# Another recorded order of the tasks in a two-layer recurrent-memory transformer, with the x blocks asked for ahead of the first V weights

## The chip, the cores and the metric

The kernel runs on one core of one Trainium2 chip. The metric is the device time of one execution in microseconds (us); lower is better. The core has five engines that run their own instruction streams in order and wait for each other by semaphores: PE (TensorE, matrix products; its weight loads are listed apart as PEld), DVE (VectorE), ACT (ScalarE), POOL (GpSimd) and SP (SyncE). DMAs are asked for ("issued") by SP and by POOL here, and are carried out by 16 DMA engines that both share. SP and POOL are queues too: an instruction that has to wait holds up everything behind it on its engine.

## The reference

All tensors are bf16. With x of 2048 rows by 512 columns, the output is

```
x = x + A(layernorm(x));  x = x + B(layernorm(x))
x = x + A(layernorm(x));  x = x + B(layernorm(x))      # the same weights again
```

A is an attention with a recurrent memory. The rows are cut into 64 segments of 32. For each segment in turn, 8 memory rows and the segment's 32 rows form h (40 rows); each of 32 heads of 128 columns has q = h Wq, k = h Wk, v = h Wv, p = softmax of the masked q k / sqrt(128), o = p v; the heads' o times Wo gives 40 rows, of which the first 8 are the memory of the next segment and the other 32 the output. So the segments follow one another strictly. B is a gated layer: (sigmoid(x w_gate) * (x w_up)) w_down with 1792 inner columns. Wq, Wk, Wv and Wo have 4.2 MB each.

## The kernel before

**Steps.** The two attention layers run interleaved: step t (0 to 69) treats segment t of layer 1 and segment t-6 of layer 2 (names `j` = 0 and 1). Steps 0 to 5 have layer 1 alone, with 40 columns of h and 14 columns of layer 2's first x rows beside them. A step is built by `emit_step`. Its heads are taken in groups g0 to g5 of 6, 6, 6, 6, 6 and 2. Per group: **QK** (line 868, matrix products of 3 heads' q and k at a time, two such halves `w0` and `w3`), a cast of it to SBUF on ACT (`qku`), **SC** (line 904, the scores), the softmax (DVE lines 918, 923, 925, ACT line 928 with the exponential, DVE lines 930, 932, 939), **PTR** (line 950, transposes of p), copies on ACT or DVE, **PVM** (line 976, p times v), a cast on ACT (`otsb`), and **WO** (line 995, times Wo, adding into one bank for the whole step). At a step's end DVE copies the new memory rows into the next step's h (line 1008), and only then can the next step's QK start.

**V.** v of the x rows is not made in the step. Each block of 128 x rows (16 blocks, 4 segments each) is normalised (`layernorm_T`, lines 582 to 595: statistics and scaling on DVE, one power on POOL, a transpose on PE), and a **V pass** (line 635: four matrix products of 512 columns with one eighth of Wv, "piece" 0 to 7) makes 128 rows by 4 heads of v. The result is cast by ACT or DVE to a staging buffer, written to a scratch in DRAM (`scr`, line 1224 on SP or POOL) and read back per step into `vsb`. The 16 or so rows that depend on the memory, or lie next to it, are made inside the step by **strips** (line 762, 32 matrix products of 512 columns, of which four run at once in column groups); these are cast to `sst` and moved by DMA to `vsb`. Blocks 2, 3, 4, 5, 7, 8, 10, 11, 13 and 14 are done ahead ("boot"), so V passes are the work that PE has while it waits for weights or for a softmax.

**Weights.** `load_weights` asks on SP for Wv in 8 pieces of 512 KB, for Wq and Wk in 6 pieces each (heads 0-2, 16-18, 3-8, 19-24, 9-15, 25-31) and for Wo in 12. Piece k of Wv is asked for only when piece k-2 has landed (`tk.after`). w_gate, w_up and w_down of the gated layer (`wg`, `wu`, `wd`) come by POOL, 256 KB at a time.

**Order.** A planner holds some 14,000 tasks. It does not decide the order: the order is recorded in a packed text, `SEQUENCE` (line 53), together with one bit for every task that two engines can do (ACT or DVE for a copy, SP or POOL for a DMA):

```
code = lzma.decompress(base64.b85decode("".join(SEQUENCE.split())), ...)
left = list(range(len(T)))
order = [T[left.pop(q)] for q in struct.unpack_from(f"<{len(T)}H", code)]
...
    tk.on = tk.eng[code[2 * len(T) + k // 8] >> k % 8 & 1]
self.replay(order)
```

`replay` goes through that order with the planner's own durations. From it come which buffer a task gets, which PE task a 256 KB load on POOL waits for (`pace`), and where `warm` puts filler matrix products (line 1214, tile `hot`) into the bank of a task that the planner expects late. `run` (line 1199) then emits the tasks in that order; each engine's stream is the order cut to its tasks.

Of the kernel before, what the change touches and what calls it, by code (L numbers as in the profile page):

```python
# [1293 lines left out]
```

## Time and profile before

| | |
|---|---|
| median of 3 runs | 1747.63 us |
| lowest and highest | 1746.31 and 1748.25 us |
| profiled execution | 1747.1 us from its first to its last instruction, clock granted in full |
| PE busy | 1733.4 us (99%) |
| DVE, ACT, POOL busy | 1248.4 (71%), 1128.5 (65%), 859.0 us (49%) |
| DMA | 273.41 MB, mean 156 GB/s; 285 and 320 GB/s in the first two fortieths of the span |

The page gives no time of the profiled execution other than its span; the span is 0.5 us under the median of the runs. In the tables of the profile "x12" is a number of instructions, "L635" a line of the kernel, `bank<-wv_sb,xvf` what is written from what. Matrix products overlap, so that a busy PE is not yet a PE at its full rate: what counts is the distance from one start to the next, for example 32 products of 512 columns in 7.07 us (line 635 at 13.28 us), that is 0.216 us each.

### The profile page before, as it was taken

The numbers are of one execution on the slowest core, as the hardware profiler recorded it, in microseconds if no ns is written. First come the engines' busy times: TensorE is split into PE (matmuls) and PEld (weight loads), VectorE is DVE, ScalarE is ACT, GpSimd is POOL, SyncE is SP. The second block draws the span as 40 slices with busy tenths as digits, with TensorE's granted clock in tenths as the row PEclk, the third lists the DMA queues.
The fourth block names the chain that finished last, engine by engine and source line by source line (L and its number), as shares of the span: only waits on it lengthen the run. The fifth ranks groups of instructions, "written<-read, shape, count | busy, mean of one in ns | idle before, by whom it ended". The sixth has DMA issues, their size and how long they took to land.

```text
span 1747.1 us, 91842 instructions
## 1 busy us (share of the span) xinstructions
PE 1733.4 (99%) x39162; PEld 1491.8 (85%) x39162; DVE 1248.4 (71%) x4208; ACT 1128.5 (65%) x3119; POOL 859.0 (49%) x1367
## 2 busy tenths in 40 slices
PE   9999999999999999999999999999999999999998
PEld 4688789889898988989888888989888888988886
DVE  5677777677767776786777767776777776767676
ACT  3576777566666766666666666666665666666564
POOL 5624345635544554445445554544455364454543
PEclk9999999999999999999999999999999999999999
DMA  8935355645645555545555464545455464554644
GB/s 285 320 100 155 109 151 161 195 113 153 174 130 163 156 159 143 165 125 164 152 148 158 136 184 128 166 138 153 132 174 166 139 174 128 144 156 131 178 120 134
DMA packets 145583, 273.41 MB, mean 156 GB/s; under 512 B 39686, under 2 KB 86018, under 8 KB 145174
## 3 DMA queue, kind: packets, MB, share of 16 engines
q0 software_dynamic: 72944, 198.79, 39.8%
q1 hardware_dynamic: 72230, 68.75, 13.3%
q8 instruction: 307, 5.03, 1.2%
q14 instruction: 102, 0.84, 0.2%
HBM read 221.78 MB, written 27.07 MB: 142 GB/s over the span
## 4 chain that ended last, share of the span: by engine, by line
PE 94%; DMA 3%; DVE 1%; SPq 1%; issue 1%; POOL 0%; ACT 0%; POOLq 0%; ACTq 0%
PE bank L868 34%; PE bank L995 17%; PE bank L1097 12%; PE bank L762 8%; PE bank L635 6%; PE bank L1120 6%; PE bank L904 4%; PE bank L976 4%; PE bank L950 2%; PE bank L595 1%; PE bank L1214 1%; DMA wk_sb<-in_A_Wk_dram 1%; DMA wo_sb<-in_A_Wo_dram 0%; PE bank L1065 0%; DMA scr<-wu 0%
## 5 line engine op out<-in xcount | busy, mean ns | idle before, releaser
L868 PE MATMUL bank<-hT,wq_sb 128*128 128x80 bf16 (+3 forms) x8960 | 616.4, 198 | 1.0 <-DVE hT L1008 0.3
L868 PE MATMUL bank<-hT,wk_sb 128*128 128x80 bf16 (+3 forms) x8960 | 616.3, 198 | 0.8 <-DMA wk_sb<-in_A_Wk_dram 0.6
L1228 ACT CAST qku<-bank 128x480 bf16<-128x480 f32 (+4 forms) x770 | 384.7, 508 | 223.7 <-PE bank L868 194.6
L868 PEld LDWEIGHTS <-wq_sb 128*128 128x128 bf16 x8960 | 454.2, 99 | 32.1 <-issue 15.1
L868 PEld LDWEIGHTS <-wk_sb 128*128 128x128 bf16 x8960 | 446.9, 99 | 1.1 <-DMA wk_sb<-in_A_Wk_dram 0.7
L995 PE MATMUL bank<-otsb,wo_sb 128*128 128x80 bf16 (+1 forms) x8960 | 360.2, 198 | 2.2 <-DMA wo_sb<-in_A_Wo_dram 1.3
L918 DVE TENSOR_TENSOR st<-bank,cst 40x240 f32<-40x240 f32 (+3 forms) x768 | 280.5, 368 | 113.2 <-PE bank L904 97.5
L995 PEld LDWEIGHTS <-wo_sb 128*128 128x128 bf16 x8960 | 336.6, 99 | 15.5 <-DMA wo_sb<-in_A_Wo_dram 2.0
L1228 ACT CAST otsb<-bank 128x480 bf16<-128x480 f32 (+3 forms) x420 | 200.2, 483 | 83.4 <-PE bank L976 52.8
L1090 POOL DMA_DIRECT2D wu<-in_B_w_up_dram x217 | 166.5, 768 | 170.0 <-PE bank L950 36.4
L1114 POOL DMA_DIRECT2D wd<-in_B_w_down_dram x217 | 156.9, 723 | 182.0 <-PE bank L1120 39.6
L1224 POOL DMA_DIRECT2D vsb<-sst x351 | 178.2, 512 | 129.6 <-ACT sst L1228 64.7
L1089 POOL DMA_DIRECT2D wg<-in_B_w_gate_dram x217 | 166.4, 767 | 138.1 <-PE bank L1097 56.7
L928 ACT ACTIVATE st<-st 80x240 f32<-80x240 f32 (+3 forms) x420 | 159.2, 381 | 58.0 <-DVE st L925 54.8
L1097 PE MATMUL bank<-xnT,wg 128*128 128x128 bf16 (+2 forms) x1784 | 171.5, 218 | 0.0
L1097 PE MATMUL bank<-xnT,wu 128*128 128x128 bf16 (+2 forms) x1784 | 171.1, 218 | 0.0
L930 DVE TENSOR_REDUCE small<-st 80x6 f32<-80x240 f32 (+3 forms) x420 | 151.5, 363 | 23.4 <-ACT st L928 20.2
L1220 ACT ACTIVATE ptsb<-bank,small 120x160 bf16<-120x160 bf16 (+3 forms) x430 | 156.6, 386 | 17.2 <-PE bank L950 10.7
L904 PE MATMUL bank<-qku 128*128 128x80 bf16 (+1 forms) x2240 | 162.7, 197 | 1.0 <-issue 0.9
L925 DVE TENSOR_TENSOR st<-st,small 80x240 f32<-80x240 f32 (+3 forms) x420 | 155.0, 370 | 5.7
L939 DVE TENSOR_TENSOR pb<-st,small 80x240 bf16<-80x240 f32 (+3 forms) x420 | 154.1, 370 | 5.7
L923 DVE TENSOR_REDUCE small<-st 80x6 f32<-80x240 f32 (+3 forms) x420 | 152.5, 364 | 6.2
(108 smaller groups left out, 2554.1 us busy)
## 6 DMA issues: line engine op xcount, KB each, us to landing
wg<-in_B_w_gate_dram POOLq DMA_DIRECT2D x220, 256.0 KB, 4.2
wu<-in_B_w_up_dram POOLq DMA_DIRECT2D x220, 256.0 KB, 4.2
wd<-in_B_w_down_dram POOLq DMA_DIRECT2D x220, 256.0 KB, 3.9
vsb<-scr SPq DMA_DIRECT2D x137, 66.0 KB
scr<-vst SPq DMA_DIRECT2D x90, 96.0 KB
vsb<-scr POOLq DMA_DIRECT2D x93, 66.0 KB, 3.4
vsb<-sst SPq DMA_DIRECT2D x179, 32.0 KB
vsb<-sst POOLq DMA_DIRECT2D x169, 32.0 KB, 2.8
```

What stands on the lines that cost most here:

```text
L868: nc.tensor.matmul(o_ap, lhsT=W[:, c, h * P:(h + 1) * P], rhs=mv(c), start=(c == 0), stop=(c == DC - 1))
L904: nc.tensor.matmul(s_all(SB)[:, w0 + i, :], lhsT=fview(qku[:, i, 0, 0:1], [(1, P)]), rhs=qku[:, i, 1, 0:ncol], start=True, stop=True)
L918: pl.add("DVE", dve_ns(n, True), lambda gsz=gsz, hs=hs, st=st, SB=SB, pj_=pj_, npj_=npj_, mk=mk, idx=idx: nc.vector.tensor_tensor(out=st[p ...
L928: pl.add("ACT", act_ns(n), lambda hs=hs, st=st: nc.scalar.activation(out=st[pr, hs], in_=st[pr, hs], func=ACTF.Exp, scale=self.scale), r=s ...
L995: nc.tensor.matmul(WB[:, c * ncol:(c + 1) * ncol], lhsT=self.wo[:, h, c * P:(c + 1) * P], rhs=otsb[:, hl, 0:ncol], start=(h == 0 and c == ...
L1089: pl.add("POOL", 760, lambda wg=wg, fs=fs: nc.gpsimd.dma_start(out=wg[:], in_=self.wgv[:, :, fs]), r=[("wo", self.H - 1)], w=[gk] + bt, la ...
L1090: pl.add("POOL", 760, lambda wu=wu, fs=fs: nc.gpsimd.dma_start(out=wu[:], in_=self.wuv[:, :, fs]), r=[("wo", self.H - 1)], w=[uk] + bt, la ...
L1097: nc.tensor.matmul(gu[:, 2 * i + k, 0:n], lhsT=W[:, c, i * P:(i + 1) * P], rhs=xnT[:, c, rw], start=(c == 0), stop=(c == DC - 1))
L1114: pl.add("POOL", 760, lambda wd=wd, ip=ip: nc.gpsimd.dma_start(out=wd[:], in_=self.wdv[:, 2 * ip:2 * ip + 2, :]), w=[dk] + (["boot"] if se ...
L1220: nc.scalar.activation(out=dst, in_=src, func=ACTF.Copy, scale=by)
L1224: {"SP": nc.sync, "POOL": nc.gpsimd}[tk.on].dma_start(out=got[1], in_=got[2])
L1228: nc.scalar.copy(out=dst, in_=src)
```

## The change

Nothing but the text `SEQUENCE` differs: 92 lines of packed text become 88.

```
 SEQUENCE = r"""
-;BKuib6o%lfB&)8j78VFm3*TORJaEeTpTegcj@45cPG=tDu9Cop`gL7BsLuS#OcT}UGbOE%Rvw4_#4%#$D8H!O&97}fvKE=gc~
...
+-XmYACJ&^@_Q*%Pqd)VfD(Os7%#QMrvJwasc?e7tW4e|DX`7=(P4&9b1jfW|}nyY`GtB?m|%9YiB{%_E6Z!fQiku2zXKR#fd!bV
...
 """
```

Both texts unpack to an order of the same 13,976 tasks, and can be compared as lists:

- **Where.** Only the front differs. On PE the last 3750 of 4202 tasks stand in the same order; the first of them is a task of step 7 that starts at 205.84 us in the profile. The other engines' orders agree from about the same place on. 191 tasks change their engine: 50 DMAs go from SP to POOL, 36 from POOL to SP, 59 copies from ACT to DVE, 46 from DVE to ACT.
- **The first requests on SP** (x4 is block 4 of x, 128 KB; v0 is piece 0 of Wv, 512 KB; m the memory rows; q, k, o pieces of Wq, Wk, Wo by heads; S a write of v to the scratch):

```
before  v0 x4 x3 v1 x14 x2 v2 m v3 x0 v4 v5 x5 v6 S x11 x7 v7 x8 x10 q16-18 x1 S S q0-2 x13 S k0-2 k16-18 S S S S q25-31 ...
after   x4 x3 x14 x2 v0 x5 v1 v2 x0 v3 v4 x11 v5 v6 x7 (mask) v7 m x1 x10 q0-2 x13 S S k16-18 x8 S S S S q25-31 S k0-2 S S q16-18 ...
```

- **Weights.** MB asked for ahead of a piece (SP and POOL together, in the recorded order), and the PE work recorded ahead of its first use (number of matrix products times their distance in the profile; fillers not counted):

| piece | MB ahead, before | after | PE work ahead, before (us) | after (us) |
|---|---|---|---|---|
| v6 | 3.94 | 4.06 | 10.40 | 11.49 |
| v7 | 4.79 | 4.72 | 13.22 | 13.44 |
| q 16-18 | 5.78 | 9.84 | 31.63 | 32.08 |
| q 25-31 | 9.22 | 7.90 | 41.05 | 39.92 |
| k 3-8 | 17.11 | 16.98 | 47.88 | 48.79 |
| o 0-2 | 19.56 | 18.83 | 54.49 | 59.29 |
| o 28-30 | 23.05 | 23.06 | 62.57 | 65.16 |

  On SP 24 writes of v stand ahead of most Wo pieces before, and 17 to 19 after. The first piece of Wo of 384 KB is the 61st request on SP before, and the 55th after. The V writes of the strip that is done ahead for block 0 stand from place 32 on before, behind q 16-18, q 0-2, k 0-2 and k 16-18; after, the first stands at place 30, behind q 0-2 and k 16-18 alone.
- **V passes.** In PE's order the V passes of block 13 with pieces 0, 1 and 2 stand in step 1 before and in step 0 after, so that step 0 has 23 V passes for 20, and step 1 none for 3. Steps 2 and 3 keep three and two. Two transposes of the layer norm stand at the end of step 3 before; after, one stands at the end of step 2 and one within step 3.
- **Start.** On DVE the first block's scaling stands behind the statistics of the second block before, and behind those of the second and third after. On POOL six clearings of buffers stand ahead of the first power after, none before.
- **Step 1.** On DVE a cast of a strip stands inside the step's softmax instructions before; after, ACT has it, and DVE has one cast to `kx` (0.23 us for this kind in the profile) inside them.
- **Step 7.** Of the 18 DMAs that fill its `vsb`, 10 are on POOL before and 8 on SP; after, 6 and 12. Between them on POOL stand five 256 KB loads for the gated layer before (issued at 201.21 to 208.02 us), of which four stand further ahead after.

More of the change, by code (lines that the diff above doesn't have):

```diff
@@ new lines @@
+!(`Ye}I4@U$IQaXEDjRGy!`PtL<i9-G13$hzV;?YvxzU_S%nj>}5AQt<$S)u+*SpZ(LQM?zaW5{YqNmQd}nP$PmtFilvq1+MOc7%LF6`h89JsjYs{wA_7TQq#b=5HArnYUIM?S_dSG4<lx0EcBu9?D*W=p`L%*#6#G{VU`^b>?vuPW
+6FiQT0!o_J)`NB!&iWBJ7<-7W26m&)A{(k@T2PFDvwsi1<s;*OJ`cXJRspxb{AL}sBs<zM;vt6=4K+>$M1I={iIvqlt;m6<6NWG@c)WETY9+BE#O0H_t}=!myNXLLQCJ6+lj*5Z6sp>5l4ztM>LwnwdZ_#_EfBSEupcg*~zZ_QFM{)
+@`HP}1mfWJ0>Za_618ryvEIm*?v4sbyAHTO(4kRDNRWZ@6+6HSX&@pw0wB*@7xHfjY!|*acCX;aw$amNxA|6z2{v6~8fECFmNK3b&14Ofrsv1G;1qZn5cXO*>>Y5$+tT}K-96&O*xgT#msf(}43%&knWSPq*tfFRMX0D42q5u6fm2Q
@@ new lines @@
+LK`)`+63>On?wcKGu@zlif|B$FN#s6_lh@`FBkq<2Kb=Rhobh6`>F;T=i{w`3ywB-Qn`W?HbZ8CD(aEXXj{H4Fa9z48>;ovo4<kBuXA0n09Gv<4!-;r-yn9{%3>_OA5nENe1<B8ep#imFD|F6_Hr+^Twxu33RbWVk(XASy!a2{f-Tr
+AW>b|eXpw9D3&Nv}IgL}6bp8e=^7LiWRNL}ne&9H^&vDTVBW&bC4lOp_zv$9pMGX^avS%vNsquy;Zv$oUjjlzC73v4AraD#(9BGH|&;4x*8q3v<*`G=Qyq)KZ)2Q0>5Hq8k6CdC6F@3je=4i^|R14i$+`wjMgqIDu>{W&!IuPGnUo7
+gdB(33EB4OT7HC@m0{tU}|JN5(0|bv<kS%65vr#%lByC;<^lXa4if%*c(t3QQ!etqPsja}hd|olAFRtln#FduWYJp^9UTJw%KJS7~L8u+@x@%)*aKMW@tw#pX;We%UBo7+{m0cCt%KL=b9;1aH0&*{}?0@+pAGYaJ}az!hHz*<%pZN
@@ new lines @@
+pr4VF;F-%N(THuG?YdD#XXT<2S_yx4uOccUb0Gj5+o~e$2X@v&);U$VhSbpmwxSnfrZmYbSrptcr&c6Sr9%|#CMAIX70;Q<&cf%G1t764=dvGUkcA*U{mDl++gsubaC;Qy4qrDF+u*61pBa-=#-x{6Rn&Q5cNo~jJ4~D;+1ZOyep`g
+U)34u>l986h48THSR)W)v5GJ|Op&V-2_nbH3@n;2Rl^;|T#B|6T5{}t>oBItCzxen&U7cpt<-j~{cQ8H7XCC~c+49JGV0PV<l51B892ThAs4!KvFJSB+w)us>=`JX9hO{ec%~0HwI>!Mg!I6tj`4@qkI2{+&NLS>{lbCVIi@`&96OC
+Ksd7Bz;<T>}3gcss26gO8$hFDw{<^a2$Mi=YC=}}I5qyxo2%4oZR*~ih<gzzy(t|yE)oo?)QPzOY6A9*bOg&{6V$#_AoR>+Q{G&(e%4ot=S{R>J0s0Lj(YN%yZV}dxK3l$ExEJ7^A(I?WC1aHJs$ENz#IFFh&k8pB)C%N5+H<t9O~L
+)KNW2jj<l|%33G-f=+r1mSr#pe`t_fK*-LdH`cdg>DqJIUV4`5GgsewM4l}UI_)VS8qk>^>CFuH5jemNW+vGQP;$dU78GZ6Z`3>^33wEc|@W8IoN>02q}hAE>=M^l=Vg+nKqh>-n84zHRiGI%?DXFH$s%3=<q#WvG5Mj-wVA>4kQd7
@@ new lines @@
+E03qH%+7lEbuG6>X$)nTif;glWDfcr%_t<yVSGzte(o?dg|VaP^Tb$|kiqvHfy6jB=owPwa<Pfk5`9R~^mH2A$obd@{uKt_-nVge&An&Glpq98)I%lixOVlKLxmi7atClf*WkE!>E*y>Pw268owasqt!;Rs1*dV2?WIX9sIlCBx90f
+1}DRp@r7FcGRnw`Jj)!=TjlL3S~6HDwZCCtM*p7hS_2wCt*rKVOZ8a`)U^F4$^Z~rUi|KBDHh}_2!-eH1nezsg7_$$9G<l6luG_<=%RqdpQFoj<QViy}XZh)c&hk(=6vqPrX{pQ31G1pzd>u20KD=?OT}$T?MUIZm{8trMaMXK=d40
+4F4?tj+LeJDjAAJO&@DVXL{%~gJ$Y+Cr`z`)vxh566DphvD6X;ZV*>4Dj^QtkoYE}#zyL7Rwu*xjA(I71j~LgMdaPn%1mV9?%3wgUar^*b#k)=qaYM(R}USBBS?&uT_CNd&fUJl5N`{mFwx_)Bep`E!{Zwik@{k-pNw1ri5&o3sGd%
@@ new lines @@
+oIch|Z^k9B<)JD8i50euasKL0-2nwG<{V;o+qlz_)qhSD2wj?OZA@Z=n#3<=SVpsWcqRQ!ieZ+W8j*5DSF0^+fovKte0yt<@fpUq_HtCfYwzTxL;L+~xetKx{uISdgfiYq{Dfv4%V5)zn*>dFaT1NTPGfyx%F<^50zfA399^#v|=oY
+JS;vS#7uNj?OTI711f_)k{Q4vs(i7pE*vQL>`7rO$QdS2Lb{*O+28Nktw^?a7^R{M<>wu{lkuTbt7?^o@hoef^L8f<8yv@j0Ge{)f4ZQZG^l@h%wt+W$jJ!S893L7{gA#G!NQG-APtD*|S{)a!JSjxNTIRie5b`T#{ykncPBCLBa9_
+etRG8<caqUs2`DaijyvXz-C9l~pJE8gery6H4APFM)W*fr{>@)X%+?n@>s8{GilrF!Ei6aMoEynJAF8fmwp2$B+vzYXtsBCy&HybpBnuMsMx-D|dgM@7~4&BaZv5i5^JEIm$=YWY^A0u>bsT+j`kAGB5qi*QzGAxYmQ$`caYl456T3
@@ L145 @@
+Jcd+-{c%-Eou@Wp{BtK{_Pl_en!PErvz@amS1+`ykBNt^=2cKl{L9VQ*deej!w02=K6_B-QHHsvzLjv5vAj86<ukdVK`0o?0$%k{AO=ps#3!%bxi_<JIU7li63j0^_G=vFOX0ntNZaTWax;FXW&$U{V&TyHd0%cy;QUXQ-Z~Nb+cW-
+p6DcpO{b2Iuy>_{GhWQj9ENV&WP2iTHn%|5z9Q)z*(fa1M&L(Pvm)M8J%l2&DTOxvkRNogEtz|i~Kb*ms=EY8>woN%l?95--S~5QQ(*wRLsB$B{$Tpp9Ly)v56QLIaGi+J<Mu1dl?r?0q6MfPDqVtEgi~s
 """
```

160 lines of the change are left out of this document (69 added, 91 removed).

## The prediction

> **What bounds the kernel now.** I read the page first: engines, then the slices.
>
> ```profile
> span 1747.1 us, 91842 instructions
> PE 1733.4 (99%) x39162; PEld 1491.8 (85%) x39162; DVE 1248.4 (71%) x4208; ACT 1128.5 (65%) x3119; POOL 859.0 (49%) x1367
> PE   9999999999999999999999999999999999999998
> DMA  8935355645645555545555464545455464554644
> ```
>
> PE is the bound nearly everywhere; DMA is full only in the first two slices (87 us). An order adds and removes no PE work, so it can only win or lose PE's idle time. The orders differ up to 205.8 us; hence the busy time by stage for that stretch.
>
> ```profile
> core 0: us, PE busy (x) PEld busy (x) DVE busy (x) ACT busy (x) POOL busy (x), PEclk, DMA share, GB/s
> 10.20:25.70 15.50, 13.14 (x70) 6.08 (x69) 8.79 (x26) 5.82 (x11) 8.82 (x21) 1.00 0.92 302
> 25.70:44.40 18.70, 18.70 (x136) 8.55 (x136) 11.44 (x31) 8.64 (x21) 12.75 (x26) 1.00 0.92 314
> 44.40:62.00 17.60, 16.90 (x294) 10.66 (x292) 10.19 (x28) 7.85 (x23) 13.92 (x27) 1.00 1.01 364
> 62.00:79.70 17.70, 16.31 (x287) 10.73 (x287) 10.87 (x38) 10.25 (x34) 7.10 (x14) 1.00 1.00 317
> 79.70:96.50 16.80, 16.76 (x495) 13.89 (x494) 11.55 (x42) 12.30 (x47) 8.13 (x15) 1.00 0.55 156
> ```
>
> Up to 79.7 us (the end of step 0) the DMA share is 0.92 to 1.01 and PE has holes; after it DMA has room. Which DMA ends the holes stands in the waits of PE up to 215 us, and how long it took in the chain:
>
> ```profile
> PE bank L635 <- DMA wv_sb<-in_A_Wv_dram: 2.4, 2, 1.9
> PE bank L995 <- DMA wo_sb<-in_A_Wo_dram: 1.3, 3, 0.6
> PE bank L868 <- DMA wk_sb<-in_A_Wk_dram: 0.6, 1, 0.6
> ```
>
> ```profile
> 18.17 7.47 DMA wv_sb<-in_A_Wv_dram
> 51.15 10.87 DMA wk_sb<-in_A_Wk_dram
> 69.99 8.54 DMA wo_sb<-in_A_Wo_dram
> ```
>
> The timeline places them. These are the piece v7, the last k piece, the last large o piece, and the first QK of step 1:
>
> ```profile
> 25.69 1.04 PE L635 MATMUL bank<-wv_sb,xvf 128*128 128x512 bf16 x4 [1.91 <-DMA wv_sb<-in_A_Wv_dram]
> 62.06 0.27 PE L868 MATMUL bank<-hT,wk_sb 128*128 128x54 bf16 x4 [0.56 <-DMA wk_sb<-in_A_Wk_dram]
> 78.58 0.84 PE L995 MATMUL bank<-otsb,wo_sb 128*128 128x40 bf16 x20 [0.62 <-DMA wo_sb<-in_A_Wo_dram]
> 79.70 0.26 PE L868 MATMUL bank<-hT,wq_sb 128*128 128x54 bf16 x4
> 94.53 0.20 PE L950 MATMUL bank<-cst,pb 66*128 66x66 bf16 x1
> ```
>
> My yardstick is PE's idle so far: the time minus the PE work recorded ahead (the counts of the change, at the distances between starts: 0.216 us for a product of 512 columns, 0.025 for 54 or 40). It is 25.69 - 13.22 = 12.5 us at v7, 62.06 - 47.98 = 14.1 at k 3-8 (its k products stand 0.1 behind the first use), 79.70 - 63.07 = 16.6 at step 1.
>
> **The change part by part.**
>
> *Start.* The first block was asked for at 1.33 behind 512 KB and its statistics began at 4.86; now it is asked for at 0.81 with nothing ahead. Gain at least 0.52, and at most 0.52 plus 512 KB at 302 GB/s (1.7), less 0.9 for the third block's statistics (0.69) and sums (0.18) that DVE now does before the first scaling: 0.5 to 1.3 us. It is covered at v7, though: that piece has 4.72 MB ahead instead of 4.79, so I let it land at 25.69 again, with 13.44 of work ahead. Idle there 12.25: gain 0.2. If v7 lands 1 us later, the next bound (13.2, below) still takes it up.
>
> *Wq and Wk.* k 3-8 has 16.98 MB ahead for 17.11. At the same landing, 48.89 us of work ahead leave an idle of 13.2 instead of 14.1. The pieces asked for later (q 16-18, with 4.06 MB more ahead) are a rival below.
>
> *Wo and the three V passes.* A V pass is 4 x 0.216 = 0.86 us; three moved into step 0 make the work ahead of o 28-30 65.16 for 62.57. It has 23.06 MB ahead for 23.05. If it lands at 78.58 again, step 1 begins at 79.70 again: gain 0, with 2.6 us more work done. If Wo no longer holds, the idle grows from 13.2 only by what is left of the 2.5 us between 62.06 and 79.70 without the Wo holes (0.38 + 0.65 + 0.77 + 0.15 between starts), about 0.55: step 1 at 65.66 + 13.75 = 79.4. With k earlier too, and v7 alone as floor, 65.66 + 12.25 + 0.55 = 78.5. I take 79.4 (gain 0.3; ends 0 and 1.2): DMA is full from 44 to 79.7, and the bytes are the same, so the landings are nearest to what they were. What is gained on SP is five writes fewer ahead of Wo.
>
> *Step 1.* It loses its three V passes: PE work 15.85 becomes 13.26. But they covered a softmax. DVE's own chain in this step:
>
> ```profile
> 82.51 0.40 DVE L918 TENSOR_TENSOR st<-bank,cst 40x240 f32<-40x240 f32 x1 [2.86 <-PE bank L904]
> 84.65 0.68 DVE L1230 CAST sst<-bank 128x512 bf16<-128x512 f32 x1
> 93.78 0.23 DVE L930 TENSOR_REDUCE small<-st 40x2 f32<-40x80 f32 x1 [0.40 <-ACT st L928]
> 94.23 0.23 DVE L939 TENSOR_TENSOR pb<-st,small 40x80 bf16<-40x80 f32 x1
> ```
>
> It runs from 82.51 to 94.46, 11.95 us, and PE's last transpose starts 0.07 later: the chain is just covered now. It loses a cast (0.60 between starts) and gains one of 0.23, so 11.6 us; if its idle times (0.20 and 0.40) and a 0.13 copy go as well, 10.85. With 2.81 from the step's start to it and 0.07 + 2.02 from its end to the next step (96.55), the step takes 15.75 to 16.5 us instead of 16.85. Gain 0.35 to 1.1; I take 0.7. PE then waits for DVE, where it waited for nothing; what is late next is DVE's line 939 of the last group.
>
> *Steps 2 to 6.* Two transposes of 0.22 us filled the hole at step 3's end (the holes at the ends of steps 0 to 2 were 0.44 us of fillers each); now one fills half of that of step 2, and step 3's opens. -0.44 + 0.22 = -0.2. The other swaps are of neighbours on PE with the same work between: 0, with +-0.5 for engines changed.
>
> *Step 7.* DMAs into its `vsb` move from POOL (0.51 us each, with 256 KB loads between) to SP. PE's holes ahead of PVM there are 0.24, 0.26 and 0.39 between starts, so 0 to 0.9; the fillers near them wait for ACT, which the move does not touch. I take 0.2, nearest to the one wait of 0.2 that the profile gives to a DMA there.
>
> *Queues.* 50 DMAs go to POOL and 36 leave it: 14 x 0.55 = 7.7 us more on POOL in 200, where it is busy half the time, and 14 fewer on SP. POOL's fullest stage is 44.4 to 62 (13.92 of 17.60), inside the DMA bound; its cover is that the weights there come by SP.
>
> Sum: 0.3 + 0.7 - 0.2 + 0.2 = 1.0 us (start and k are inside the 0.3). The profiled execution goes from 1747.1 to 1746.1; it lies 0.5 under the median, so 1747.6 - 1.0 = **1746.6 us**. From the ends: 0 + 0.35 - 0.7 + 0 = -0.35, and 1.2 + 1.1 + 0.3 + 0.9 = 3.5.
>
> **The rivals.**
>
> *The landings alone decide (no gain).* If DMA is the bound to 79.7, moving requests between queues moves no landing: step 1 at 79.70, its softmax at the slow end, 0.35 - 0.2 = 0.15 gained: 1747.5. For it: shares of 1.00 and 1.01. Against it: SP asked for the first large Wo piece only at 60.20, behind 24 writes that wait for casts. [...]
>
> *More than the sum.* The DMA share of 0.70 in the first 10 us and 0.92 to 44 leaves some 3.5 us of DMA time unused. If the new order of requests fills 1 us of it, v7, k and Wo all land 1 us earlier, step 1 begins at 78.4, and with the good ends of steps 1 to 7 the gain is 1.3 + 1.1 + 0.3 + 0.9 = 3.6, more with 2 us filled: 1743.5. Against it: the bytes ahead of v7 and of the last pieces are unchanged.
>
> *Slower: SP stands at the strip's write.* SP runs in order. Before, the first write of the strip waited for a DVE cast and was issued at 31.12, with 8.09 MB asked for on SP; now it stands at place 30 with 7.29 MB ahead, and q 25-31, k 0-2 and q 16-18 behind it. The strip's products stand at the same work (15.17), so it can't go much before 31. Then 0.80 MB less are asked for by then; where DMA runs dry, that is 0.80 MB at 314 GB/s = 2.5 us for every later piece. k lands at 64.6, idle 15.7, step 1 at 81.9 (2.2 later); less 0.7 of step 1: 1747.6 + 2.2 - 0.7 = 1749.1. It decides from the point where k lands after 62.9. If the writes behind it (five more in a row, 0.63 us each) hold the pieces as long again, 1752. For it: a share of 0.85 already between 30 and 40 us.
>
> *The change doesn't do what it says*: not possible in the order itself; the number of fillers and the waits of 256 KB loads follow the planner and may shift.
>
> **How the numbers follow.** Forecast 0.44 (its own range 1745.0 to 1747.3); landings alone 0.18; more 0.18; slower 0.18; the rest 0.02. Faster or slower by 0.2% (3.5 us, about what a measurement of this kernel tells from no change) means under 1744.1 or over 1751.1: nearly all of "more" lies below, 0.16, plus 0.01; of "slower" the part with the doubled hold, 0.12; the rest, 0.71, is the same. The range reaches into both: 1743.4, short of two pieces filled, to 1750.4, between the single and the double hold.
>
> **What would show it.** First V pass before 9.8 us; a wait of over 2 us at v7; k 3-8's first products at 61.5 to 63; waits for Wo shorter than 1.3 us in all; step 1's last transpose waiting 1 to 2 us for DVE; from step 8 on the old course, shifted. Wrong if DMA's share between 25 and 44 us falls under 0.85, or if POOL's V writes or `vsb` reads in steps 0 to 2 end PE's waits.

## The result, and the profile after

The new order is slower: 1755.27 us (median of 11 runs, 1751.43 to 1759.04) against 1748.25 us (1746.16 to 1754.47). The ratio is 1.0035, 95% interval 1.0022 to 1.0048: 6.1 us, between 3.8 and 8.4 (the two medians lie 7.0 us apart). Forecast were 1746.6 us and a range of 1743.4 to 1750.4. The profiled execution took 1758.06 us (span 1756.3), 2.8 above the median, so its own numbers overstate the loss a little.

The page, the lines shown of before:

```profile
span 1756.3 us, 91642 instructions
...
PE 1724.8 (98%) x38943; PEld 1492.5 (85%) x39160; DVE 1255.2 (71%) x4221; ACT 1126.2 (64%) x3106; POOL 865.2 (49%) x1381
...
PE   8999999999999999999999999999999999999998
...
DMA  8935355635645555545555464555465464554544
```

PE is still the bound nearly everywhere, and its first slice is no longer full. (Some 220 matmul records are missing here: PE's busy time and its count of products are not to be compared. Its weight loads are all there, and where a product's record is missing a task's start is taken from them.) The stages of before, cut at the same times:

```profile
core 0: us, PE busy (x) PEld busy (x) DVE busy (x) ACT busy (x) POOL busy (x), PEclk, DMA share, GB/s
10.20:25.70 15.50, 12.96 (x64) 5.81 (x65) 7.55 (x19) 6.92 (x15) 5.59 (x12) 0.95 0.83 261
25.70:44.40 18.70, 17.74 (x123) 8.07 (x126) 11.63 (x33) 8.82 (x21) 14.40 (x27) 0.95 0.89 282
44.40:62.00 17.60, 16.66 (x297) 10.62 (x297) 8.93 (x24) 7.88 (x23) 12.60 (x24) 1.00 1.05 391
62.00:79.70 17.70, 17.36 (x238) 10.55 (x241) 12.62 (x42) 10.24 (x27) 13.04 (x25) 1.00 0.99 327
```

Two columns tell the story. DMA's share falls from 0.92 to 0.83 and 0.89 in the first two stages: (302 - 261) x 15.5 + (314 - 282) x 18.7 = 1.2 MB that were not moved, 3.4 us at the 359 GB/s that the next two stages have on average. From 44 us on DMA is full, as before (shares of 1.05 and 0.99, for 1.01 and 1.00). These two stages moved (391 - 364) x 17.6 + (327 - 317) x 17.7 = 0.65 MB more than before's, so about half of what was lost was made up by 79.7 us, and no more. And PEclk, which was 1.00 everywhere, is 0.95 in both. PE's waits up to 215 us, then the chain, then the timeline:

```profile
PE bank L631 <- DMA wv_sb<-in_A_Wv_dram: 3.4, 4, 2.0
PE bank L972 <- DMA scr<-vst: 1.5, 1, 1.5
PE bank L991 <- DMA wo_sb<-in_A_Wo_dram: 1.5, 2, 1.1
```

```profile
3.72 5.57 DMA wv_sb<-in_A_Wv_dram
...
9.38 4.57 DMA wv_sb<-in_A_Wv_dram
...
13.96 5.20 DMA wv_sb<-in_A_Wv_dram
...
19.22 7.49 DMA wv_sb<-in_A_Wv_dram
...
51.40 12.82 DMA wk_sb<-in_A_Wk_dram
...
72.13 10.29 DMA wo_sb<-in_A_Wo_dram
```

```profile
26.75 2.23 PE L631 MATMUL bank<-wv_sb,xvf 128*128 128x512 bf16 x8 [0.86 <-DMA wv_sb<-in_A_Wv_dram]
...
64.27 0.28 PE L864 MATMUL bank<-hT,wk_sb 128*128 128x54 bf16 x4 [0.17 <-DMA wk_sb<-in_A_Wk_dram]
...
82.47 0.67 PE L991 MATMUL bank<-otsb,wo_sb 128*128 128x40 bf16 x20 [0.37 <-DMA wo_sb<-in_A_Wo_dram]
```

The chain now begins with four pieces of Wv: v1, asked for at 3.72 us (before 2.34), then v3, v5 and v7, each asked for in the moment in which the one two ahead of it has landed, v7 at 19.22 (18.17). The longest wait of PE, 2.05 us, is for v6. v7 is first used at 26.75 (25.69), k 3-8 at 64.27 (62.06), o 28-30 at 82.47 (78.58). Step 1 begins at 83.42 (79.70), step 2 at 99.54 (96.55).

All runs at a glance. The columns are the first use of v7 and of o 28-30, the start of steps 1, 2, 5 and 7 (us, in the one profile), and the ratio to before by the timed runs:

| run | v7 | o 28-30 | step 1 | step 2 | step 5 | step 7 | ratio (95%) |
|---|---|---|---|---|---|---|---|
| before | 25.69 | 78.58 | 79.70 | 96.55 | 148.91 | 194.03 | |
| after | 26.75 | 82.47 | 83.42 | 99.54 | 151.95 | 199.95 | 1.0035 (1.0022-1.0048) |
| e1 after, steps 4 on as before | 25.28 | 81.41 | 82.36 | 98.90 | 151.58 | 197.29 | 1.0032 (1.0022-1.0042) |
| e2 before, steps 5 on as after | 23.35 | 76.59 | 77.71 | 94.44 | 147.07 | 194.76 | 1.0004 (0.9994-1.0014) |
| e3 after, v0 and v1 first | 24.96 | 79.52 | 81.23 | 98.19 | 150.55 | 196.57 | 1.0026 (1.0016-1.0035) |
| e4 before, x first | 28.29 | 79.36 | 80.68 | 97.58 | 149.86 | 195.16 | 1.0012 (1.0002-1.0022) |
| e5 after, V passes back | 25.90 | 83.87 | 85.42 | 104.78 | 158.84 | 204.57 | 1.0054 (1.0042-1.0066) |
| e6 before, V passes early | 24.85 | 77.27 | 79.95 | 98.30 | 150.86 | 196.63 | 1.0026 (1.0017-1.0035) |
| e7 e3 with q, k early | 24.20 | 78.42 | 79.66 | 97.00 | 149.51 | 196.32 | 1.0027 (1.0014-1.0040) |
| e8 before, q, k late | 25.08 | 79.53 | 80.57 | 98.18 | 150.96 | 198.89 | 1.0017 (1.0008-1.0025) |
| e9 before, three V pieces | 22.80 | 77.49 | 78.59 | 95.27 | 147.51 | 193.32 | 0.9996 (0.9987-1.0005) |
| e10 after, three V pieces | 21.91 | 77.87 | 79.62 | 96.73 | 149.13 | 194.19 | 1.0007 (0.9998-1.0016) |
| e11 e6 without fillers | 24.61 | 76.28 | 78.95 | 96.58 | 148.75 | 195.44 | 1.0019 (1.0010-1.0029) |
| e12 e10 with a filler | 21.76 | 77.41 | 78.51 | 94.63 | 146.99 | 193.70 | 0.9996 (0.9985-1.0007) |
| e13 after, step 6's DMAs moved | 23.73 | 80.01 | 81.12 | 97.24 | 149.60 | 195.18 | one run, 1748.57 us |
| e14 e7 with e9's and e12's edits | 24.45 | 77.75 | 78.69 | 95.74 | 148.10 | 193.45 | 1.0013 (1.0004-1.0022) |

One profile is good to 1 or 2 us only: before and e2 have the same order up to step 5, and v7 was used at 25.69 and 23.35; after, e1 and e13 have the same order up to step 4, and step 2 began at 99.54, 98.90 and 97.24. Their means differ by 3.1 us at step 2 (98.56 and 95.50).

What DMA had moved in the first 32 us sorts the sixteen profiles into two groups. In nine (before, e2, e6, e7, e9, e10, e11, e12, e14) it was 9.1 to 9.4 MB, and o 28-30 was first used at 76.3 to 78.6 us. In the other seven (after, e1, e3, e4, e5, e8, e13) it was 8.0 to 8.5 MB, and the use came at 79.4 to 83.9 us.

### The profile page after: what moved, and what is told of

It is laid out like the page before. It is cut to its first block, busy times and chain, and to the rows that moved or that the text cites. A ratio compares the mean times of both kernels' runs of the same rounds, so it can differ in the third digit from the quotient of the medians.

```text
span 1756.3 us, 91642 instructions
## 1 busy us (share of the span) xinstructions
PE 1724.8 (98%) x38943; PEld 1492.5 (85%) x39160; DVE 1255.2 (71%) x4221; ACT 1126.2 (64%) x3106; POOL 865.2 (49%) x1381
## 4 chain that ended last, share of the span: by engine, by line
PE 87%; DMA 5%; DVE 4%; ACT 2%; SPq 1%; issue 1%; POOL 0%; POOLq 0%; ACTq 0%; DVEq 0%
PE bank L864 31%; PE bank L991 17%; PE bank L1093 11%; PE bank L758 8%; PE bank L631 5%; PE bank L972 4%; PE bank L900 4%; PE bank L1116 4%; PE bank L946 2%; DMA wv_sb<-in_A_Wv_dram 1%; DVE st L914 1%; SPq L507 1%; PE bank L591 1%; DMA wk_sb<-in_A_Wk_dram 1%; DMA wo_sb<-in_A_Wo_dram 1%
## 5 line engine op out<-in xcount | busy, mean ns | idle before, releaser
L1216 ACT ACTIVATE ptsb<-bank,small 80x160 bf16<-80x160 bf16 (+3 forms) x427 | 155.4, 386 | 17.0 <-PE bank L946 10.4
```

Source lines behind the costliest of these rows:

```text
L1216: nc.scalar.activation(out=dst, in_=src, func=ACTF.Copy, scale=by)
```

## The experiments

**In which steps is the loss?** Two spliced orders.

```
e1  order: tasks of after up to the first QK of step 4, then the rest in the order of before
e2  order: tasks of before up to the first QK of step 5, then the rest in the order of after
```

> The order is that of after up to the first QK of step 4, and from there on that of before. If the loss sits in the start and again in steps 5 and 6, this keeps the start's part alone: in the profiles step 4 begins 3.1 us later than before (132.68 for 129.55), so the time should be 3 us over before, about 1751, and step 7 should begin 3.1 us late instead of 5.9. If the loss is not local to those steps (a slower state that the whole run carries), it stays at 5 to 7 us.

> The other half: the order is that of before up to the first QK of step 5, and from there on that of after. If steps 5 and 6 lose by their own order, the profile shows again a wait of P.V for DMAs of about 1.5 us near 187 us and the time is 1.3 to 2 us over before. The stall of 1.04 us in the middle of a QK that after showed in step 5 should not come again if it is chance: then step 6 begins 0.6 us late at most. If these steps lost only because they began late, nothing is lost here: 0 to 0.3 us.

e1 kept 1.0032 of 1.0035: nearly all of it is in front of step 4, more than the 3 us expected (5.6, 3.8 to 7.3). e2 lost 0.7 us (-1.0 to 2.4): what steps 5 and 6 cost by their own order is too small to be told from nothing. The stall of 1.04 us in a QK did not come again; another of 1.4 us did, in a strip ("issue": PE waited for nothing that the profile shows). The splice also brought five filler products at 161.19 us (1.08 us) that neither order has there.

**The first eight requests.**

```
e3 (after)   - x4 x3 x14 x2 v0 x5 v1 v2 ...
             + v0 x4 x3 v1 x14 x2 x5 v2 ...
e4 (before)  - v0 x4 x3 v1 x14 x2 v2 ... x5
             + x4 x3 x14 x2 v0 x5 v1 v2 ...
```

> After, with only its first eight requests on SP put into the order of before: v0 x4 x3 v1 x14 x2 x5 v2. Theory of the V chain: piece v1 is asked for 1.4 us earlier, and v3, v5 and v7 follow (each asked for when the one two ahead of it has landed), so v7 lands at 25.6 instead of 26.7, and as DMA is the bound up to 80 us, the last Wo piece lands 1 to 2 us earlier than in after (80.5 to 81.5): 1 to 2 us under after. Theory of the writes: SP stands at writes of v between 23 and 33 us whatever the start, the last Wo piece lands at 82 to 82.5 again, and the time is that of after within 0.5 us.

> Before, with only its first eight requests put into the order of after: x4 x3 x14 x2 v0 x5 v1 v2. Theory of the V chain: v7 is asked for at 19.2 instead of 18.2 and lands at 26.7, step 1 begins 1 to 2 us later than before, and the time is 1 to 2 us over before. Theory of the writes: the pieces of Wq, Wk and Wo are held by other things on SP, v7 lands within 0.4 us of 25.7 and the time is before's within 0.5 us. If the early x blocks help (an earlier first V pass), it is up to 1 us under before.

With x first, before gets 2.1 us slower (0.3 to 3.8), v1 is asked for at 3.71, v7 at 20.26, and v7 is first used at 28.29. With v0 and v1 first, after gives back 0.0009 x 1748 = 1.6 us, v7 is asked for at 17.73 and the last Wo piece is used at 79.52 for 82.47. The signs are what the chain of V pieces says; the sizes are a quarter to a third of the loss, and that of e3 is not clear of noise (its interval overlaps after's). e3 also isn't a clean return: x comes later in it (asked for at 1.33 us for 0.81), the planner put 33 fillers ahead of the first V pass for after's 20, and that pass began at 11.18 us for 8.74. In e3 DMA's share between 24 and 32 us was still 0.82, where before has 1.04.

**The V passes.**

```
e5 (after)   V passes of block 13, pieces 0-2, their casts and writes: step 0 -> step 1, casts on ACT
e6 (before)  the same: step 1 -> step 0, casts on DVE
e11          -                if tk.idx in fill:
             +                if tk.idx in fill and tk.idx not in (648, 575, 577):      (in e6)
```

> After, with the three V passes of block 13 (pieces 0, 1, 2), their casts and their writes put back into step 1, where before has them; SP's order of weights stays. Theory of the landings: step 0 ends with the last Wo piece whatever PE has done by then, so step 1 begins as in the other runs with after's front (81.2 to 83.4 us), but step 1 is then 16.85 us long instead of 16.1 to 16.5: step 2 begins 0.3 to 0.7 us later and the time is 0 to 0.7 us over after's. Theory of the passes: the 2.6 us of work put into step 0 filled no hole; then step 1 begins 1 to 2.5 us earlier than in after and the time is 1 to 2 us under after's.

> Before, with those three V passes moved into step 0 (at 61 to 65 us of work, where after has them at 60 to 62) and with after's engines for their casts; nothing else. Theory of the landings: Wo lands as before (76.6 to 79.4 us in the runs with this order), step 1 begins within 0.5 us of before and is 0.3 to 0.7 us shorter: 0 to 0.7 us under before. Theory of the passes: step 1 begins 1 to 2.5 us later and the time is 1 to 2 us over before.

> The run of before with three V passes moved into step 0, without the 16 filler products that the planner had put into step 1 in their place (3.4 us: ahead of the scores of g4, of P.V and of Wo of g0). The fillers write nothing that is used. If the fillers were the price, step 1 is 15.8 to 16.5 us long instead of 18.35 and the time falls from 0.26% over before to within 0.05% of it. If PE had to wait there anyway (softmax, or vsb), the idle takes the fillers' place and the time stays within 1 us of 0.26% over.

e5 got slower still. With 2.6 us less work in step 0, PE waited 4.0 us for Wo instead of 1.5, and the last piece was used at 83.87: in after's order the landings set the end of step 0, whatever PE has done.

```profile
PE bank L996 <- DMA wo_sb<-in_A_Wo_dram: 4.0, 4, 1.6
```

Its time says nothing of the V passes, though: behind those waits the clock stood at half for 3.4 us (0.92 from 82 to 84 us, 0.50 to 86, 0.73 to 88), and in step 2 the planner had put eight fillers (1.84 us) that after hasn't. Of the landings e6 shows the same from the other side (o 28-30 at 77.27, step 1 at 79.95 with 2.6 us more work done), and yet is 4.5 us slower: step 1 took 18.35 us. Its timeline shows why, in the row of the filler products:

```profile
90.00 2.86 PE L1215 MATMUL bank<-hot 128*128 128x512 bf16 x13
```

The planner expected PE to wait there and filled the time. Without the 18 fillers of step 1 (e11) PE waited 1.03 us at that place instead of working 2.69 us on them, but the clock then fell to half (0.51 from 92 to 94 us, 0.64 from 94 to 96), and the ratio was 1.0019 for 1.0026: a share of the price, within the errors. In before's order the three passes are worth more in step 1, where they keep PE at work under the softmax (16.85 us with them; 17.63 in e11, the half clock included).

**q 16-18 and k 0-2.**

```
e7 (e3)      x10 [+ q16-18] q0-2 x13 [+ k0-2] S S k16-18 x8 ...  (both were among the strip's writes)
e8 (before)  x10 [- q16-18] x1 ... S [- k0-2] k16-18 ... q25-31 S [+ k0-2] ... S [+ q16-18] S q9-15 ...
```

> The order with after's body and before's first eight requests (v0 and v1 early), and in addition q 16-18 and k 0-2 asked for ahead of the V writes (behind x10 and x13, about 20 and 22 us) instead of among the strip's writes (33.9 and 31.9 us). If the rest of the loss is DMA time that ran dry between 24 and 32 us because SP stood at writes, DMA's share there goes from 0.8 to over 0.95, the last Wo piece lands at 77 to 78.5 us instead of 79.5, and the time is 1 to 2 us under that run, that is 1747.5 to 1749.5 for 1746.9 before. If those pieces only take the place of others in a DMA that is full later on anyway, Wo lands at 79.5 again and the time stays at 1751.

> Before, with only q 16-18 and k 0-2 asked for late, as in after: among the strip's writes at 33 to 36 us instead of 19.8 and 26.5 us. If DMA runs dry for that, its share between 20 and 32 us falls from 1.0 to about 0.85, 768 KB at 340 GB/s come 1 to 2 us later, and the time is 1 to 2 us over before. If not, within 0.5 us of before.

e8 lost 3.0 us (1.4 to 4.4). DMA's share between 24 and 32 us fell to 0.85 (before 1.04), the large pieces of Wq, Wk and Wo behind them were asked for 1.1 to 1.4 us later, and PE stood for one of them:

```profile
58.86 0.27 PE L869 MATMUL bank<-hT,wq_sb 128*128 128x54 bf16 x4 [2.53 <-DMA wq_sb<-in_A_Wq_dram]
...
60.41 1.73 PE L1215 MATMUL bank<-hot 128*128 128x512 bf16 x8
```

The second row is again the planner's: eight fillers, 1.57 us from their start to the next product's, that before hasn't, and behind them PE waited for no Wo piece any more. So up to 1.6 of the 3.0 us can be theirs and not the late pieces'.

e7 brought that share to 1.00 and the last Wo piece to 78.42, as expected, and step 2 to 97.00; but its times (1.0027) are not better than e3's (1.0026). Eight of its 12 executions had a granted clock below 1, and it has e3's 33 fillers. Nor is the share between 24 and 32 us the price by itself: in e10 and e14, below, it is 0.87 and 0.72, and the last Wo piece was used at 77.87 and 77.75, since more had been moved before.

**Three pieces of Wv under way.** The wait in the chain, loosened:

```
-            ..., [("wv", h0 - 8)] if h0 > 4 else [])
-            if h0 > 4:
-                tk.after = pl.writer[("wv", h0 - 8)]
+            ..., [("wv", h0 - 12)] if h0 > 8 else [])
+            if h0 > 8:
+                tk.after = pl.writer[("wv", h0 - 12)]
```

> Before, with one size changed: piece k of Wv is asked for when piece k-3 has landed, instead of k-2, so that three pieces can be under way. Theory of the V chain: v2 no longer stands on SP for v0, v7 is asked for at 15 to 16.5 us instead of 17 to 18.2 and lands 1 to 2 us earlier than in before (25.6), DMA's share between 8 and 16 us goes from 0.7 to over 0.85, and since what follows is bound by DMA, the time is 1 to 2 us under before. If the chain only shares a DMA that gives no more (first pieces land later as the others come earlier), v7 lands within 0.5 us of before and the time is before's within 0.7 us.

> After, with the same change: three pieces of Wv under way. If the x blocks cost by lengthening the chain, this gives back more here than in before: v7 is asked for at 16 to 17.5 us instead of 19.2, the last Wo piece lands 1 to 2 us earlier, and the time is 2 to 3 us under after's, that is 0.2% over before instead of 0.35%. If not, it stays at 0.3 to 0.4% over before.

e10 is the run that settles most: with after's order, engines, buffers and fillers all unchanged, 4.9 of the 6.1 us are gone (1.0007 for 1.0035, and the intervals do not meet). SP asked for v7 at 15.61, v7 was in use at 21.91 without a wait, and the two early stages moved more than before's:

```profile
10.20:25.70 15.50, 15.50 (x105) 7.14 (x103) 9.71 (x24) 8.33 (x19) 8.63 (x18) 1.00 1.02 332
25.70:44.40 18.70, 18.70 (x164) 9.24 (x166) 11.61 (x33) 8.98 (x22) 14.10 (x27) 1.00 0.95 328
```

Since SP runs in order, all that stands behind the V pieces came earlier too: q 25-31 at 27.16 us for 32.33, k 3-8 at 46.25 for 51.40. e9 shows that before had little to gain from it (0.9996): v7 was used 2.9 us earlier, but Wo at 77.49. That is not far from the 76.59 to 78.58 that this order gave anyway.

**The clock.** In e10 the last waits for Wo stand close together (1.16, 0.24, 0.39 us), and the clock falls right behind them. e12 puts four filler products (0.86 us) ahead of them:

```
-            fill = self.pl.warm(order)
+            fill = self.pl.warm(order); fill[372] = (<the bank that the V pass 372 takes>, 16)
```

> The run of after with three pieces of Wv under way, and in addition 0.86 us of filler products (four of 512 columns into a bank that is overwritten) ahead of the V pass at 73.17 us, so that PE comes later to the Wo products for which it then waits 1.3, 0.4, 0.55 and 0.25 us. In that run the clock fell to 0.5 for 3.4 us right behind those waits, and the first QK of step 1 were 0.18 us apart instead of 0.10. Theory of the clock: waits that come close together cost the clock, not only their own time; with the fillers in their place the clock stays at 1.00, step 1 begins at 79.6 again and step 2 at 95.8 instead of 96.7, most runs show a clock of 1.0, and the time is 0.8 to 1.2 us under that run (1.0002 of before for 1.0007). Rival: the clock falls by chance, and not for the waits; then it falls here too, or the time is the same or 0.9 us longer for the fillers.

The stretch of 3.4 us in which the waits lie, and the next, in e10 and then in e12:

```profile
75.40:78.80 3.40, 1.61 (x51) 1.41 (x51) 0.12 (x1) 0.58 (x2) 2.05 (x5) 0.94 1.01 357
78.80:82.20 3.40, 3.40 (x74) 3.06 (x75) 0.19 (x1) 0.20 (x1) 3.18 (x7) 0.56 0.84 271
```

```profile
75.40:78.80 3.40, 2.68 (x79) 2.15 (x76) 0.53 (x2) 0.64 (x3) 1.93 (x4) 1.00 1.05 374
78.80:82.20 3.40, 3.40 (x135) 3.25 (x135) 0.84 (x3) 1.79 (x8) 3.40 (x8) 1.00 0.75 230
```

PE busy 1.61 us of 3.4, then a clock of 0.56 and 74 products; busy 2.68, then 1.00 and 135 products. Step 1 took 16.12 us for 17.11, 10 of 12 executions had the full clock for 1 of 11, and the ratio went from 1.0007 to 0.9996 (the intervals overlap). After shows the same behind its wait of 2.05 us for v6:

```profile
20.30:23.70 3.40, 1.35 (x7) 0.50 (x6) 1.25 (x3) 1.32 (x4) 0.58 (x1) 1.00 1.04 323
23.70:27.10 3.40, 2.54 (x11) 1.19 (x10) 0.93 (x5) 0.59 (x1) 0.00 (x0) 0.55 0.85 269
```

**Step 6's DMAs.**

```
e13 (after)  POOL: 1441 1445 1444 1570 <256 KB load> 1446  ->  1443 1441 1445 1444 1446 <256 KB load>;  SP: - 1443  + 1570
             (1441-1446: the second strip's rows for step 6; 1570: step 7's read of vsb)
```

> After, with three DMAs of step 6 and 7 moved: the last 12 KB of the second strip's rows stand ahead of the 256 KB load on POOL and of step 7's own read (which goes to SP), and one 48 KB piece is on POOL, as in before. If the wait of 1.5 us of P.V in step 6 comes from that queue, it falls under 0.5 us and step 6 adds 0.4 to 0.6 us of idle instead of 2.1. If it comes from something else (a cast, or SP's own writes), it stays at 1 to 1.6 us. It also shows the front of after a second time: v7 first used at 25 to 27 us, step 1 at 82 to 84 us, the clock at 0.5 behind the wait for v7.

The wait of P.V in step 6 was gone, and the step took 23.2 us (24.7 in after). But it was also absent in e3, e5, e10 and e14, which have after's order there, and 0.3 to 0.8 us long in e2, e7 and e12. That these DMAs cause it is therefore not shown; it comes in some executions. The one execution of e13 took 1748.57 us, under all eleven of after (1751.43 at the least) and within before's range on that chip (1745.00 to 1754.89). One execution decides nothing, but it leaves open that these DMAs carry a part of the loss.

**Everything together.**

```
e14          e7's order, with e9's edit and e12's filler
```

> The four remedies together on the body of after: v0 and v1 asked for early, three pieces of Wv under way, q 16-18 and k 0-2 ahead of the V writes, and the 0.86 us of fillers ahead of the V pass at 73 us. If each remedy takes away a loss of its own, DMA's share stays over 0.9 from 4 to 60 us, the last Wo piece lands at 76 to 77 us (77.4 with two of the remedies), step 2 begins at 93 to 94.5 us and the time is 1 to 2 us under before. If they all heal the same hole in DMA's first 32 us, step 1 begins at 78.5 us again, bound by the bytes, and the time is before's within 0.7 us.

1.0013: not better than each remedy alone. PE waited for no weights any more up to step 1, yet it began late: 33 fillers stood ahead of the first V pass, which started at 10.80 us, where e12 has 20 and 8.19 us, since x comes later when v0 and v1 go first (as in e3). Step 1 began at 78.69 us, as in e9 and e12. So these are not losses that add up: it is one shortfall in what DMA moves in the first 32 us. No version beat before by more than its uncertainty (e9 and e12: 0.9996).

## Why the prediction was wrong

- **Start: the step that failed.** It was right that the first V pass would come earlier than 9.8 us (8.74; in before 10.23). It was wrong to let v7 "land at 25.69 again" because as many bytes were ahead of it. In these two profiles its landing followed its request and not the bytes: v7 took 7.47 us from request to landing before and 7.49 after, and the request hangs on v1's through two landings. v1 lost 1.38 us to the x blocks and x5, v7's first use 1.06. The other profiles bear out the request (17.1 to 17.9 us with before's start in e2, e6, e8 and e11, 18.4 to 19.8 with after's in e1, e5 and e13), while the landings scatter by over 2 us; and with the requests of Wv alone moved, to 14.41 in e9 and 15.61 in e10, v7 was used at 22.80 and 21.91. The "next bound" that was to take it up moved too, as it stands on SP behind the same pieces.
- **Wq and Wk.** 61.5 to 63 us forecast, 64.27 measured. The count of MB ahead (16.98 for 17.11) hid when these MB were asked for: at 28.2 us SP had asked for 7.0 MB instead of 8.0. k 3-8 itself was asked for at 51.40 for 51.15, and took 12.82 us for 10.87: what stood ahead of it was late.
- **Wo and the V passes.** "DMA is full from 44 to 79.7, and the bytes are the same, so the landings are nearest to what they were" is the argument that carried the number, and it was read the wrong way round: where DMA is full to the end, what it did not move in the first 32 us comes late at the last piece (the two groups of profiles above). Step 1 at 83.42 for 79.4. Nor were the bytes the same. The count of 23.06 MB for 23.05 goes by the recorded order, but POOL runs ahead of SP: when SP asked for o 28-30, POOL had asked for 4.0 MB in after and for 3.4 in before, 0.6 MB more, nearly all of it writes of v, which at 359 GB/s are an estimated 1.7 us. That step 0's end does not mind 2.6 us more work was right for after's order (e5).
- **Step 1.** Gain 0.7 us forecast (15.75 to 16.5 us long), 0.73 measured (16.12). The wait for the softmax that was to come with it can't be seen: the profile lists no wait of PE in this step, as the planner's fillers stand there (seven products from 92.92 to 97.2 us). Steps 2 to 4: 52.41 us for 52.36, forecast 0.2 lost. Step 7: 20.09 for 20.26, forecast 0.2 gained. These small terms came out.
- **Steps 5 and 6** were given nothing but +-0.5 and took 2.9 us more in this profile (1.04 of it the stall in a QK); over the runs 0.7 (e2). Most of the 2.9 is chance: with after's order these two steps took 45.1 to 48.0 us in eight profiles (mean 46.4), with before's 45.1 to 47.9 in seven (mean 46.0).
- **The rivals.** "SP stands at the strip's write" had the right place and sign and its condition came true (k later than 62.9). Its price was too low (1749.1, or 1752 with the doubled hold), and its chance of 0.18 too small. Up to k it was nearly met (64.27 for 64.6); what it lacked came behind k, in the landings of Wo (step 1 at 83.42 for its 81.9). The rival of more than the sum put 3.5 us of DMA time as unused; its own shares, 0.70 for 10.2 us and 0.92 for the 34 us behind, give 5.8. e9 filled much of it (9.4 MB moved in 32 us for 9.1), and gained nothing that can be told from noise. The forecast's own sign of being wrong, a DMA share under 0.85 between 25 and 44 us, did not show (0.89): the share fell lowest ahead of 25 us (0.83). "The landings alone decide" did not come true either: the last large piece of Wo was used 3.9 us later (82.47 for 78.58), though SP and POOL remained the only two queues, and SP asked for it at 72.13 us for 69.99.
- **The clock was in no term.** It had been 1.00 in every stage of before's profile. Of after's 11 executions 4 had the full clock, of before's beside the experiments 87 of 118; an execution at 0.999 was some 1.8 us longer (before beside e1: 1748.6 for 1746.8). The profiles show why. From 7 us on and up to the last microseconds of the span, before's, at 1.000, has no stretch at half the clock; those of e1, e3, e5, e7, e9, e10 and e11, at 0.999, show one of 3.4 us; and after's, at 0.998, has two (from 24.1 and from 1689.8 us, a clock of 0.50 in both). A stretch costs at most 1.7 us, half of its length. By these steps of 0.001, after's 11 executions had 10 such stretches and before's 118 had 37, 0.9 and 0.3 each; so about 1 of the 6 us is the clock, by this estimate.
- **What stays open.** The profiles give 3.1 us for the front, and e2 0.7 for steps 5 and 6; the times say 5.6 for the front and 6.1 in all, each +-2. The rest is not placed. Of the 9.2 us between the two profiled spans, 3.3 lie behind step 7, where the orders agree; 2.0 of these came at once in step 67, with the second stretch at half the clock (the row below). How the loss divides between the x blocks (1.6 to 2.1), the late q and k pieces (3.0 in before with up to 1.6 of fillers, nothing measurable in after), the 0.6 MB of early V writes and the chain (4.9) can't be told either: they share one hole.

```profile
1690.00:1695.00 5.00, 5.00 (x105) 2.82 (x98) 3.49 (x10) 1.63 (x5) 0.82 (x2) 0.68 0.02 5
```

## What to carry to other kernels

Where a transfer may start only when an earlier one has landed, count not only the bytes that stand ahead, but look when the first of the chain is asked for, and at each request's own time on its queue. In this kernel's first phase, which ends with DMA full, DMA time that went unused earlier came back at the end (1.2 MB not moved by 44 us, and the last large piece of Wo used 3.9 us later), so compare the bytes moved by stage in the early part first. And before work is moved to fill a hole elsewhere, ask whether the place that it leaves then falls idle, or to half the clock (in e11 a wait of 1.03 us, and then a clock of 0.51). Where a planner adds filler work by its own forecast, look at what it added before a run's time is put down to the edit: here it did so in e2, e3, e5, e6 and e8.

## What the runs showed of the hardware

Holes of 2 us can cost more than themselves. The clock fell to half (0.50 in after from 24.06 us) for 3.4 us after a stretch of 3.4 us in which PE had been busy 1.35 us (after) or 1.61 us (e10), with no single hole over 2.05 us; a stretch with 2.68 us busy kept it (e12).

What decides is not shown: neither the length of a hole nor PE's busy share sorts these cases by itself. Before's hole of 1.91 us left PE busy for 1.50 us between 23.60 and 27.01 us, and the clock stayed at 1.00. In the 3.41 us ahead of a fall PE was busy 1.36 us in after (from 20.65 us), 1.96 us in e10 (from 74.99 us, longest hole 1.16 us), and 2.10 us ahead of after's second fall at 1689.77 us (longest hole 1.31 us).

The landing of the same requests differs by more than 2 us from one execution to the next (v7 at 25.69 and 23.35 us in before's order, 26.75, 25.28 and 23.73 in after's), so that one profile of such a start can't carry a forecast of 1 us.
